# Filling matmuls around the score gradients of a backward loop, and earlier copies of turned weights in a forward loop

## Chip, cores, metric

One core of one Trainium2 chip. The metric is the device time of one execution in microseconds; lower is better.

## The reference, cut to what matters

A gated block with its gradients, bfloat16. The time goes into branch A, a segment-recurrent attention: 2048 tokens in 64 segments of 32; each segment attends to itself and to 8 memory rows, and the memory of the next segment is the output on those 8 rows. So both the forward pass and the backward pass are 64 steps in series.

```python
for s in range(n_seg):                         # 64, serial through mem
    xs = x[:, s * 32:(s + 1) * 32, :]
    h = jnp.concatenate([mem, xs], axis=1)     # 8 + 32 rows
    q, k, v = (einsum('btd,dhe->bhte', h, W) for W in (Wq, Wk, Wv))   # 32 heads x 128
    p = softmax(where(mask, q @ k.T * scale, -1e9))
    o = einsum('bhte,hed->btd', p @ v, Wo)
    mem = o[:, :8, :]
    outs.append(o[:, 8:, :])
# out = x + A(layernorm(x)) * silu(B(layernorm(x))), B a gated MLP;
# the kernel returns out and jax.vjp(...)(grad_out) for nine inputs
```

## The kernel before

A step computes only what lies on the memory rows. The work on the 32 tokens of earlier segments is put as fill into named gaps of the chain (W0, W1, G1 to G6), in units of four heads. `t` counts down in the backward loop; a step has 3, 3 or 2 units (2 where t mod 3 is 1). `WARM` says how many filling matmuls (128x512, result unused) a gap gets.

```python
# backward step, cut to the part that the change touches
packed_half(k, bA, gox, WoT, 0);  k.copy(sg[:, 0:512], bA[:], eng='v')
packed_half(k, bB, gox, WoT, 1);  k.copy(sg[:, 512:1024], bB[:], eng='s')
gap("W0")
# ... packed_sel into pg (bank C), copied to gmT
nc.sync.dma_start(k.GOS[...], sg[:])
gap("W1")
for h in range(H):                       # score gradients of the memory rows: 32 x 8 columns
    nc.tensor.matmul(psd[...], vT[:, h, :], gmT[...], start=True, stop=True)
# ... dPT and gOst copied on ScalarE
gap("G1")
gvT = gkv(1, gOst, bdP)                  # ends on VectorE
# ... softmax gradient on VectorE; loads(t - 1): vT, Pm, Qst (2) by nc.sync
gap("G2")
packed_out(k, pm, gvT, WvT, True, False) # value projection, 64 matmuls of 320 columns
# ... load_k(t - 1) by nc.sync; four stores of dS, two by nc.sync, two by nc.gpsimd
```
```python
def gap(g):                                              # backward fill
    if g == "W0":   ride_ld(t - 1); at(turn, t, 0)
    elif g == "W1": at(turn, t, 1); at(gmem_ld, t + 1, 2)   # turn needs gqv, gor
    # ... G1 to G3
    elif g == "G4": load_xp(t - 1); at(dsoft, t, 1); at(gmem_ld, t, 0)
    elif g == "G5": at(dprob, t, 2); at(gmem_ld, t, 1)
    # ... G6
    for i in range(WARM.get(g, 0)):
        nc.tensor.matmul((bA if g[0] == "W" or g == "G1" else bB)[:], k.ident[:], WqT[:, 0, 0:512], ...)

def ld(tl, qd):                        # the loads of one unit, four units ahead of use
    # ...
    for (a, b, src, w) in k.m_src(tl, "qv", c0, c0 + 512):          # L1174, w = 1: values
        (nc.gpsimd if early and w else nc.sync).dma_start(qv[a:b, w], ...)
    k.load_x(qv, nm, k.x_src(...), nc.sync)                          # L283
    k.load_x(gor, nm, k.g_src(...), ...)                             # L283, nc.sync
    nc.sync.dma_start(Pr[0:n], ...)                                  # L1177
```
```python
def gap(g):                                              # forward fill
    FILL(g, t, at, kbatch)                               # G3: maxima, exponentials of a unit
    for i in range(WARM.get(g, 0)):
        nc.tensor.matmul((bA if g == "G4" else bB)[:], k.ident[:], Wq[:, 0, 0:512], ...)
    if g in ("G2", "G5"):                                # turn a piece of a weight on TensorE
        wt["u"] = units.pop(0); wt["p"] = bview(bA if g == "G2" else bB, ...)
        wt["u"][0](wt["p"])
    if g == "G2": turned('v', nc.sync)                   # copy to wTst on VectorE, then store
    if g == "G6": turned('s', nc.sync)                   # the same on ScalarE
```

## Time and profile before

| | kernel before |
|---|---|
| time | 5631.07 us, median of four runs (5621.08 to 5634.92); the profiled one 5632.72 |
| TensorE busy | 88% of the span; next VectorE, 42% |
| forward loop, first to last step's start | 1354.6 us in 63 steps |
| backward loop, the same | 1260.6 us in 63 steps |
| half-clock stretches in the backward loop | 48, 187 us |

A half-clock stretch is a run of the clock record at half of full speed; a step with one at its value projection is called cold below, one without it warm. The two loops are read from the trace: the start of a step is its first matmul on `hx` (forward) or `gox` (backward). The prediction below shows the windows and the timeline. One view that it tells of only in words is the list of what TensorE waited for in the backward loop (columns: us in all, times, longest):

```profile
PE gbank L1090 <- DVE gmT L1085: 47.1, 57, 1.3
PE gbank L370 <- DVE gkv L1069: 27.4, 64, 0.4
```

These are the two idle places per step, some 0.8 us before the score gradients (L1090) and 0.4 before the value projection (L370), into which the change puts matmuls.

### The profile page before, as it was taken

The numbers are of one execution on the slowest core, as the hardware profiler recorded it, in microseconds if no ns is written. First come the engines' busy times: TensorE is split into PE (matmuls) and PEld (weight loads), VectorE is DVE, ScalarE is ACT, GpSimd is POOL, SyncE is SP. The second block draws the span as 40 slices with busy tenths as digits, with TensorE's granted clock in tenths as the row PEclk, the third lists the DMA queues.
The fourth block names the chain that finished last, engine by engine and source line by source line (L and its number), as shares of the span: only waits on it lengthen the run. The fifth ranks groups of instructions, "written<-read, shape, count | busy, mean of one in ns | idle before, by whom it ended". The sixth has DMA issues, their size and how long they took to land. (4 is left out here: it accounts for less than half of the span.)

```text
span 5628.0 us, 166669 instructions
## 1 busy us (share of the span) xinstructions
PE 4974.2 (88%) x67201; PEld 3195.0 (57%) x67486; DVE 2378.9 (42%) x7485; ACT 1834.3 (33%) x5040; POOL 1566.2 (28%) x2606
## 2 busy tenths in 40 slices
PE   4988889899888775889888896999999999999999
PEld 2554555555555453556666564665566556657565
DVE  5742555555555423444445442332233223311461
ACT  2432455555555522323333331332223212301111
POOL 0000244444444303333333332342234223300000
PEclk9999999999999787989999997999999999999999
DMA  7563455556555475666666664444344334456332
GB/s 256 181 205 94 140 163 168 167 166 170 161 157 151 113 208 164 177 185 182 188 179 179 174 173 114 120 100 98 84 108 102 99 87 102 122 163 228 102 118 91
DMA packets 1007171, 835.83 MB, mean 149 GB/s; under 512 B 505131, under 2 KB 894919, under 8 KB 1003083
## 3 DMA queue, kind: packets, MB, share of 16 engines
q1 hardware_dynamic: 760275, 570.63, 35.7%
q0 software_dynamic: 92560, 149.71, 9.5%
q10 hardware_dynamic: 153564, 104.81, 6.5%
q8 instruction: 532, 8.72, 0.6%
q14 instruction: 240, 1.97, 0.1%
HBM read 511.81 MB, written 324.39 MB: 149 GB/s over the span
## 5 line engine op out<-in xcount | busy, mean ns | idle before, releaser
L1460 PE MATMUL wg<-gr,hr 120*128 120x512 bf16 (+1 forms) x2640 | 588.1, 384 | 17.3 <-DVE dST L1392 13.2
L1438 PE MATMUL g<-w,gT 128*128 128x320 bf16 x3840 | 547.9, 299 | 0.0
L1460 PEld LDWEIGHTS <-hr 120*128 120x128 bf16 (+1 forms) x2640 | 257.8, 99 | 339.5 <-issue 45.9
L1438 PEld LDWEIGHTS <-gT 128*128 128x128 bf16 x3840 | 368.6, 98 | 136.0
L251 POOL DMA_DIRECT2D r<-GOS x256 | 143.1, 564 | 794.1 <-PE r6p L1402 720.5
L370 PEld LDWEIGHTS <-gkv 128*8 128x8 bf16 x8192 | 213.6, 98 | 152.1 <-DVE gkv L1069 34.4
L90 DVE CAST wgo<-wg 128x512 bf16<-128x512 f32 x72 | 47.5, 687 | 583.3 <-PE wg L1460 292.1
L351 PEld LDWEIGHTS <-hx 128*32 128x32 bf16 x7680 | 180.1, 96 | 182.7 <-issue 30.9
L90 DVE CAST stg<-bank 128x512 bf16<-128x512 f32 x256 | 177.0, 691 | 224.2 <-PE bank L351 213.6
L661 ACT ACTIVATE xP<-xsp,xnm 120x120 bf16<-120x120 f32 (+1 forms) x704 | 239.9, 375 | 32.1 <-issue 25.6
L370 PE MATMUL gbank<-WvT,gkv 128*8 128x320 bf16 x4096 | 225.6, 396 | 27.4 <-DVE gkv L1069 27.4
L1447 DVE TENSOR_TENSOR ghacc<-ghacc,g 128x320 f32<-128x320 f32 x240 | 117.0, 487 | 277.2 <-PE g L1438 277.2
L92 ACT CAST wgo<-wg 128x512 bf16<-128x512 f32 x48 | 25.8, 589 | 635.5 <-PE wg L1460 635.5
L1405 ACT CAST gr<-r6p 120x512 bf16<-120x512 f32 (+1 forms) x176 | 103.1, 586 | 361.2 <-PE r6p L1402 339.6
L1220 POOL DMA_DIRECT2D DSR<-gdS x176 | 101.6, 577 | 419.1 <-DVE gdS L1218 370.1
L710 POOL DMA_DIRECT2D OR<-xv x163 | 93.3, 572 | 444.2 <-ACT xv L709 280.8
L672 POOL TENSOR_TENSOR xP<-xP,xrz 120x480 bf16<-120x480 bf16 x163 | 161.6, 992 | 162.1 <-ACT xP L661 108.0
L92 ACT COPY gT<-t6g 128x960 bf16<-128x960 bf16 (+5 forms) x216 | 166.8, 792 | 118.4 <-PE t6g L1421 117.9
L370 PE MATMUL bank<-Wo,oTm 128*32 128x320 bf16 x4032 | 177.7, 330 | 14.7 <-DVE oTm L579 13.5
L1218 DVE SCALAR_TENSOR_TENSOR gdS<-gdp,Dx,gPr 120x120 bf16<-120x120 f32 (+1 forms) x680 | 182.9, 331 | 0.0
L536 DVE COPY vt<-stg 8x512 bf16<-8x512 bf16 x512 | 166.1, 324 | 31.8 <-ACT stg L92 24.9
L370 PEld LDWEIGHTS <-oTm 128*32 128x32 bf16 x4032 | 138.6, 105 | 64.9 <-issue 41.0
(360 smaller groups left out, 11094.4 us busy)
## 6 DMA issues: line engine op xcount, KB each, us to landing
QVS<-stg SPq DMA_DIRECT2D x128, 256.0 KB
gqv<-QVS SPq DMA_DIRECT2D x108, 192.0 KB
vTt<-VTD SPq DMA_DIRECT2D x64, 320.0 KB
VTD<-gvT POOLq DMA_DIRECT2D x168, 120.0 KB, 3.4
OR<-xv POOLq DMA_DIRECT2D x163, 120.0 KB, 2.8
DSR<-gdS POOLq DMA_DIRECT2D x168, 112.5 KB, 3.2
dS<-DSR SPq DMA_DIRECT2D x168, 112.5 KB
P<-PR SPq DMA_DIRECT2D x168, 112.5 KB
```

The lines of the kernel that those rows point to most:

```text
L90: return nc.vector.tensor_copy(out, in_)
L92: return nc.scalar.copy(out, in_)
L251: eng.dma_start(d, src if src.shape[0] > 1 else src[0])
L351: k.nc.tensor.matmul(bank[32 * g:32 * g + 32, :], x[:, dc, :], W[:, dc, c0:c0 + 512], start=(dc == 0), stop=(dc == k.DC - 1), tile_positio ...
L370: k.nc.tensor.matmul(pm[p0:p0 + nq, 0:320], x[:, h, :], W[:, h, 320 * b:320 * b + 320], start=(first and i == 0), stop=(last and i == 15), ...
L536: nc.vector.tensor_copy(vt[p0:p0 + 8, c0:c0 + 512], sv[32 * g:32 * g + 8, b * 512:(b + 1) * 512])
L661: nc.scalar.activation(Pb[0:n, j, 0:n], sp[0:n, j, :], ACT.Exp, bias=nmx[0:n, j:j + 1], scale=k.scale, accum_out=Z[0:n, j:j + 1])
L672: eng.tensor_tensor(Pb[0:n, :, 0:n], Pb[0:n, :, 0:n], bc_last(rz[0:n], n), ALU.mult)
L1218: nc.vector.scalar_tensor_tensor(dS[0:n, j, :], dp[0:n, j, :], Dx[0:n, j:j + 1], Pr[0:n, j, :], op0=ALU.subtract, op1=ALU.mult)
L1438: nc.tensor.matmul(pg[:], ring[:, i, j, r0:r0 + P], Ws[qd][i][:, j, 320 * h:320 * h + 320], start=(i == 0 and j == 0), stop=(i == 2 and j ...
L1447: nc.vector.tensor_tensor(a if qd < 7 else gx[:, 320 * h:320 * h + 320], a, g[h][:], ALU.add)
L1460: nc.tensor.matmul(accs[dc][:], hr[0:n, tl, dc * P:(dc + 1) * P], st["g", NTL * qd + tl, i][0:n, :], start=(tl == 0), stop=(tl == NTL - 1))
```

## The change

Its intent: keep TensorE busy enough ahead of the value projection that its clock isn't halved; and in the forward loop let the copies of the turned weights hold up neither the maxima on VectorE nor the key projection.

```diff
@@ forward loop
             def gap(g):
+                if g == "G6":
+                    turned('s', nc.sync)
                 FILL(g, t, at, kbatch)
+                if g == "G3":
+                    turned('v', nc.sync)
                 for i in range(WARM.get(g, 0)):
@@
-                if g == "G2":
-                    turned('v', nc.sync)
-                if g == "G6":
-                    turned('s', nc.sync)
             return gap
@@ backward loop
-        WARM = dict(G1=1, G5=2, G6=1)
+        WARM = dict(W1=3, G1=2, G2=2, G5=2, G6=1)
@@
-                    nc.tensor.matmul((bA if g[0] == "W" or g == "G1" else bB)[:], ...
+                    nc.tensor.matmul((bA if g in ("W1", "G1", "G2") else bB)[:], ...
```

More of the change, by code (lines that the diff above doesn't have):

```diff
@@ L1288, in gap @@
                 for i in range(WARM.get(g, 0)):
-                    nc.tensor.matmul((bA if g[0] == "W" or g == "G1" else bB)[:], k.ident[:], WqT[:, 0, 0:512], start=True, stop=True)
+                    nc.tensor.matmul((bA if g in ("W1", "G1", "G2") else bB)[:], k.ident[:], WqT[:, 0, 0:512], start=True, stop=True)
             return gap
```

## The prediction

> **What bounds the kernel now.** I read the page first: TensorE is busy 88% of the span, no other engine over 42%. The change touches two loops of 64 steps each. By the first and last matmuls on their inputs, the forward loop runs from 543 to about 1918 us, mean step 21.50 us; the backward loop from 2205 to about 3486, mean step 20.01. A step is a serial chain TensorE, VectorE, ScalarE, TensorE, with filling work between its links, so I asked for the granted clock by stretch.
>
> ```profile
> core 0: us, PE busy (x) PEld busy (x) DVE busy (x) ACT busy (x) POOL busy (x), PEclk, DMA share, GB/s
> 500.00:2000.00 1500.00, 1303.84 (x23456) 820.18 (x23582) 803.08 (x2348) 786.38 (x2643) 580.27 (x829) 0.95 0.55 155
> 2200.00:3480.00 1280.00, 1134.43 (x24248) 754.07 (x24379) 592.46 (x2777) 379.29 (x1231) 420.64 (x768) 0.92 0.62 169
> ```
>
> The backward loop has the lower clock, 0.92. Two neighbouring steps of it, as windows, then what differs between them in the timeline of TensorE:
>
> ```profile
> 3046.15:3064.97 18.82, 16.77 (x386) 11.63 (x389) 8.60 (x41) 6.38 (x20) 6.62 (x13) 1.00 0.70 184
> 3064.97:3085.23 20.26, 18.38 (x395) 12.36 (x398) 10.30 (x53) 6.68 (x22) 7.13 (x14) 0.92 0.67 191
> ```
> ```profile
> 3050.77 1.00 PE L1090 MATMUL gbank<-gmT,vTt 128*40 128x8 bf16 x32 [0.89 <-DVE gmT L1085]
> ...
> 3053.36 2.35 PE L370 MATMUL gbank<-WvT,gkv 128*8 128x320 bf16 x64 [0.43 <-DVE gkv L1069]
> ```
> ```profile
> 3072.19 3.75 PE L370 MATMUL gbank<-WvT,gkv 128*8 128x320 bf16 x64 [0.43 <-DVE gkv L1069]
> ```
>
> The reader is to see that the value projection (WvT) takes 2.35 us in a step at full clock and 3.75 in the next, and that this is nearly the whole difference between 18.82 and 20.26. Step by step in the trace, all warm steps are 18.83 us (18.48 where t mod 3 is 1), most cold ones 19.95 to 20.52. The clock record has 48 half-clock stretches in this loop, 187 us in all; nearly all begin 6.0 to 7.7 us after the step's start, where the value projection is. Windows of 3.41 us around one of them:
>
> ```profile
> 2709.89:2713.30 3.41, 3.34 (x65) 2.10 (x58) 2.70 (x14) 1.20 (x4) 1.43 (x3) 1.00 0.52 151
> 2713.30:2716.71 3.41, 2.25 (x57) 1.90 (x55) 1.25 (x3) 2.30 (x8) 2.58 (x5) 1.00 0.89 233
> 2716.71:2720.13 3.42, 3.19 (x52) 1.68 (x56) 3.21 (x19) 0.00 (x0) 0.00 (x0) 0.50 0.95 315
> ```
>
> The window before the cold one holds 57 matmuls, but nearly all small: 32 of 8 columns (score gradients), some of 24 to 128. In the forward loop one step of the commonest kind reads:
>
> ```profile
> 1092.04 0.49 DVE L90 COPY wTst<-bank 128x640 bf16<-128x640 bf16 x1 [0.27 <-PE bank L295]
> 1092.45 0.65 DVE L655 TENSOR_REDUCE xmx<-xsp 120x4 f32<-120x480 f32 x1
> ```
> ```profile
> 1094.41 2.45 PE L370 MATMUL bank<-Wo,oTm 128*32 128x320 bf16 x64 [0.43 <-DVE oTm L579]
> ...
> 1101.69 0.40 PE L351 MATMUL bank<-Wk,hx 128*32 128x512 bf16 x4 [0.26 <-ACT wTst L92]
> ```
> ```profile
> 1097.33 0.27 ACT L661 ACTIVATION_READ_ACCUMULATOR xP<-xsp,xnm 120x1 f32 x1
> 1097.62 0.29 ACT L381 COPY fup<-bank 64x160 f32<-64x160 f32 x1
> ```
>
> The weight copy holds VectorE while the maxima (xmx), whose scores are long there, wait. That delays the exponentials (xP) on ScalarE, and they delay the fold copy (fup) on which the next step depends. The last line of TensorE waits for the second weight piece's copy.
>
> [...] the granted clock is 1.0 or 0.5 only, in multiples of 3.41 us. [...] Here two fillers of the forward loop start 0.22 to 0.23 us apart. [...] here a filler's record is 0.38 long at that spacing, so I count starts. [...] the reduction above begins right at the copy's end.
>
> **Part 1, the fillers.** Per backward step three are added ahead of the score gradients (place W1), one after them (G1, now two), two ahead of the value projection (G2, none before): 6 a step, 384 in the loop, each 128x512; the order of instructions on TensorE confirms the count, and nothing else moves there.
>
> Does it warm the clock? For every 3.41 us window I added up columns over granted clock, overlaps counted once. Windows that precede a cold one lie under about 0.35 of the window, others above, in both loops (5 of 293 windows backward and 6 of 378 forward are out of order). This is an estimate from the trace[...]. Sliding a window over a backward step, the share sinks to 0.16 and stays under the threshold for starts over some 2.0 of 3.41 us. Three fillers are 3 x 0.213 = 0.64 us, 0.19 of a window; two more 0.12. Put into the idle time at W1 and G2 they lift the least share in ordinary steps to 0.35 to 0.42, and the one at G1 adds 0.06 to some. So nearly every one of these cold windows should go.
>
> What it saves: the 64 steps take about 1280.5 us; 43 x 18.83 + 21 x 18.48 = 1197.8; difference 82.7. Of it 18 lie in seven odd steps: the first, two around a late transfer (gride, about 2430 us), the last four, which have little fill. There I take 5. So 65 + 5 = 70 saved.
>
> What it costs: idle before the score gradients is 0.88 to 1.06 us from the last matmul's columns; three fillers need 0.10 + 3 x 0.22 = 0.76 and fit. Before the projection it is 0.59; two need 0.54 and just fit: say 0.03 x 64 = 2 us. At G1 there is room for one only: two end at about 6.4 us after the step's start, the matmuls that follow start at 6.34 now, so 0.07 x 64 = 4.5. In some four steps the fill before W1 ends late and the fillers delay: 4 x 0.65 = 2.6. They write bank A, whose last reader finished long before, so there is no new wait. Net -61 us.
>
> **Part 2, the forward copies.** The first piece's copy goes behind the maxima of two softmaxes: these start 0.40 us earlier (0.76 in steps with t mod 3 = 1, where the copy also waited for its transposes). The exponentials can't start before the probabilities' copy (PTm) on the same engine, so gain 0.33 and 0.65; the fold copy, now 1.06 us after the last projection matmul where 0.38 is usual, follows them. Against it: two fillers ahead of the output projection write the bank that the copy reads, so must now wait for it; the projection starts 0.17 later, 0.21 earlier, 0.15 later in the three kinds of step. In the third kind, with two softmaxes, the exponentials do not bind, and the 0.15 is lost. Sum of three steps: -0.33 - 0.65 + 0.15 = -0.83.
> The second piece's copy at once: the second half of the key projection starts 0.43 to 0.64 us after the first's last matmul, where 0.19 is the usual gap of four; -0.24 - 0.45 - 0.45 = -1.14 (less, -0.81, in the last third). Some 20 threes of 1.97 or 1.64 give -37 us. But the fillers now leave the window that is poorest in columns: by the same sliding sum its share falls to 0.26 in the first kind and 0.31 in the third, some five more cold windows of 1.5 us: +8. Net -29.
>
> **Sum.** 5632.7 - 61 - 29 = 5543 us, 1.6% faster.
>
> **Rivals.** (a) The fillers lengthen the chain more than they warm it: at half clock three last 1.3 us and overrun the 0.88. For it: a busy TensorE at 88%. Against: 17 steps have no cold window, and the idle time is measured in them. It would give 5600 to 5640. (b) Faster backward steps run into transfers: share 0.62 of the queues, loads with one buffer (values, keys). For it: one late transfer already. Against: neighbouring warm steps, up to three, show no wait. It would give back 20 to 30 us: 5568. (c) The forward copies bring more cold windows than they save, as the steps may lock to six windows (20.48 us), as backward steps do now: +25, 5568. (d) Both parts come in full and no extra cold windows come: 5632.7 - 75 - 40 = 5518, just over 2%.
>
> **Range and chances.** Part 1 gives 45 to 75, part 2 gives 5 to 42, the odd transfers and run spread (5621 to 5635) some 7 either way: 5510 to 5582. Over 2% means under 5520, which needs (d): 0.17. Slower by 2% needs a mechanism that I don't see: 0.01; the rest, 0.82, is within 2%.
>
> **What would show it.** Right: backward clock about 0.97 or more, fewer than 15 half-clock stretches there, value projection 2.35 us in ordinary steps, steps of 18.5 to 18.9, score gradients still 4.6 us after the step's start. Forward: fold copy 0.3 to 0.65 us earlier in two of three steps, and no wait of the key projection for the weight copy. Wrong: steps warm but longer than 18.9 (a), new waits for transfers (b), forward clock under 0.95 (c), or the fillers there with the projection still at 3.7 us[...].

## The result, and the profile after

5564.02 us median (5556.07 to 5579.3, four runs) against 5631.07 (5621.08 to 5634.92, four runs): ratio 0.9887, 95% interval 0.9861 to 0.9913. It counts as the same, being within 2%, and is 1.1% faster. Ratios here are the mean time of one kernel's runs over that of the other's of the same rounds, so not quite the ratio of the medians.

By stretch, from the traces of both (us):

| | before | after | difference | predicted |
|---|---|---|---|---|
| forward loop | 1354.6 | 1323.4 | -31 | -29 |
| backward loop | 1260.6 | 1227.8 | -33 | -61 |
| between the loops | 308.4 | 303.1 | -5 | 0 |
| after the loops | 2161.9 | 2167.0 | +5 | 0 |
| half-clock stretches, backward | 48 (187 us) | 8 (56 us) | | under 15 |

The 5 us between and after the loops, where the kernels are the same, are within what all the traces show there (302.4 to 312.0 and 2160.5 to 2172.2 us).

The windows of the kernel after (columns as in the prediction; the second to last triple is clock, DMA share, GB/s):

```profile
500.00:2000.00 1500.00, 1321.61 (x23715) 817.80 (x23841) 807.03 (x2367) 794.88 (x2657) 580.75 (x829) 0.95 0.56 160
2160.00:3420.00 1260.00, 1156.07 (x24695) 759.39 (x24882) 591.06 (x2783) 381.40 (x1233) 424.14 (x775) 0.97 0.64 173
```

The forward step that answers to the one in the prediction (that one began at 1078.04, this one at 1066.51), then the first line of the step after it:

```profile
1080.60 0.65 DVE L655 TENSOR_REDUCE xmx<-xsp 120x4 f32<-120x480 f32 x1
...
1081.39 0.49 DVE L90 COPY wTst<-bank 128x640 bf16<-128x640 bf16 x1
...
1082.45 2.36 PE L370 MATMUL bank<-Wo,oTm 128*32 128x320 bf16 x64
...
1085.20 0.29 ACT L381 COPY fup<-bank 64x160 f32<-64x160 f32 x1
...
1087.74 2.34 PE L351 MATMUL bank<-Wk,hx 128*32 128x512 bf16 x40
```

The weight copy now comes behind the maxima, the fold copy 18.69 us into the step in place of 19.58, and the key projection runs in one piece (x40, no wait for `wTst`). Of the 0.89 us of the fold copy, 0.37 lie between the end of the output projection and the copy, near the predicted 0.33; the rest lies ahead, 0.32 of it already where the query projection starts (3.42 us into the step before, 3.10 now). So the forward part shows what was predicted.

The clock of the backward loop rose from 0.92 to 0.97. An ordinary step in the timeline of TensorE (it starts at 3053.17):

```profile
3057.79 1.00 PE L1090 MATMUL gbank<-gmT,vTt 128*40 128x8 bf16 x32 [0.25 <-DVE gmT L1085]
3060.43 2.35 PE L370 MATMUL gbank<-WvT,gkv 128*8 128x320 bf16 x64
```

The score gradients start 4.62 us into the step as before, the value projection takes 2.35. Ordinary steps are 18.90 us, or 18.54 where t mod 3 is 1. So the clock part worked as planned. But the sum of 63 such steps is 1183 us and the loop took 1228: 45 us lie in excess of it. Where, the waits of TensorE in the backward loop show:

```profile
PE gbank L1289 <- issue: 11.7, 67, 0.3
PE gvpt L1186 <- DMA gqv<-QVS: 9.7, 7, 3.9
PE gbank L1090 <- DVE gmT L1085: 7.6, 22, 0.7
PE gvpt L1186 <- DMA gqv<-QVX: 5.5, 3, 2.4
```

The idle time before L1090 went from 47.1 to 7.6 us, taken by the fillers (L1289). New are waits of up to 3.9 us for the loads of `gqv`, in the fill at W1 (`turn`, L1186). By steps, 38 us of the 45 lie in twelve such steps, ten of them with t mod 3 = 1; the other 7 in two steps around a late transfer that the kernel before has too. One such step, TensorE:

```profile
3029.97 2.34 PE L351 MATMUL gbank<-WoT,gox 128*32 128x512 bf16 x40
...
3032.67 0.59 PE L359 MATMUL gbank<-sel,gstg 128*128 128x32 bf16 x8
3034.72 0.37 PE L1186 MATMUL gvpt<-ident,gqv 120*128 120x120 bf16 x4 [1.46 <-DMA gqv<-QVX]
...
3036.86 1.24 PE L1090 MATMUL gbank<-gmT,vTt 128*40 128x8 bf16 x32
...
3041.00 3.26 PE L370 MATMUL gbank<-WvT,gkv 128*8 128x320 bf16 x64
```

TensorE idles 1.46 us for `gqv`, then does the fillers though the score gradients are overdue (they start 6.89 us into the step), and the half clock is back from 3036.08 to 3042.91 us: 3.26 us for the value projection. The step took 23.20 us at a mean granted clock of 0.85; the ordinary one above had 1.00. Of the loop's waits for `gqv` in this fill, five, 1.46 to 3.91 us long, have the half clock begin during them or within 1.4 us of their end; of the others, up to 1.58, none has. The issues of SyncE (SPq) in the same stretch, second column the length of the issue:

```profile
3027.77 1.01 SPq L1046 DMA_DIRECT2D xp<-GXP  x1
3028.88 0.59 SPq L1236 DMA_DIRECT2D GXP<-gks  x1
3029.57 2.08 SPq L1174 DMA_DIRECT2D gqv<-QVS  x4
3031.69 0.60 SPq L283 DMA_DIRECT2D gqv<-QVX  x1
3032.39 0.54 SPq L283 DMA_DIRECT2D gor<-GOS  x1
3032.97 0.43 SPq L1177 DMA_DIRECT2D gPr<-PR  x1
```

The load that TensorE waits for was issued at 3031.69, 1.7 us after the step's start, and was in use 3.0 us later, which is the usual time (from issue to the last update of its semaphore, the median of the 56 loads `gqv<-QVX` of the loop is 2.9 us, before and after alike). It is late because it was issued late, and SyncE issues one transfer right after another: from 3019.38 us on, no gap between two of its records in this stretch is over 0.2 us, so it wasn't held up by a wait either. Here the next record starts 0.04 to 0.10 us after the last, once 0.17. Counted over the loop, SyncE issues 1725 transfers, 27.4 a step, and they take 944 us plus 115 between them (0.55 us each and 0.07 between), 1059 of 1228 us. Before it was 936 + 114 = 1050 of 1261. By kind of step (t mod 3 = 0, 1, 2; t from 6 to 59 without the two around the late transfer) this was 15.7, 18.5 and 18.7 us in the kernel before, against warm steps of 18.83, 18.48 and 18.83: two of three steps leave it next to no slack. So my theory after the traces: **the change made SyncE's issuing the second bound of the backward loop.** The rival: the transfers themselves come late, the same bytes in shorter steps.

### The profile page after: what moved, and what is told of

It reads as the page before. It is cut to its first block, busy times and chain, and to the rows that moved or that the text cites. A ratio compares the mean times of both kernels' runs of the same rounds, so it can differ in the third digit from the quotient of the medians.

```text
span 5565.9 us, 167384 instructions
## 1 busy us (share of the span) xinstructions
PE 4988.2 (90%) x67526; PEld 3177.3 (57%) x67870; DVE 2372.9 (43%) x7485; ACT 1836.6 (33%) x5040; POOL 1567.2 (28%) x2606
## 5 line engine op out<-in xcount | busy, mean ns | idle before, releaser
L370 PEld LDWEIGHTS <-gkv 128*8 128x8 bf16 x8192 | 190.9, 88 | 104.3 <-DVE gkv L1069 24.6
L1421 PE MATMUL t6g<-ident,gr 120*128 120x120 bf16 (+1 forms) x2112 | 171.1, 220 | 3.6 <-DVE wgo L90 3.1
L1289 PE MATMUL gbank<-WqT,ident 128*128 128x512 bf16 x453 | 156.4, 394 | 19.5 <-issue 11.7
```

The costliest lines, as they stand in the source:

```text
L370: k.nc.tensor.matmul(pm[p0:p0 + nq, 0:320], x[:, h, :], W[:, h, 320 * b:320 * b + 320], start=(first and i == 0), stop=(last and i == 15), ...
L1421: nc.tensor.transpose(pt[:, i - i0, j, :], st["g", u, i][0:n, j * P:(j + 1) * P], k.ident[0:n, 0:n])
```

## The experiments

Every run was correct. e1 to e4 ran on one chip, r_after and e6 to e8 on a second, e10 to e13 on a third, each group with runs of the kernel before among them.

### The two parts apart: e1_fill_only, e2_fwd_only

```diff
 e1: kernel before, with only
+        WARM = dict(W1=3, G1=2, G2=2, G5=2, G6=1)      and the bank bA for W1, G1, G2
 e2: kernel after, with
+        WARM = dict(G1=1, G5=2, G6=1)
```

> The backward part of the change alone (three fillers at W1, one more at G1, two at G2); the forward loop is that of the kernel before. If the two parts add up, this saves what the backward loop saved in the trace of the whole change: 33 us of its loop, so about 5599 us, ratio 0.994, with late loads of gqv and gor stalling TensorE in some ten steps as in the whole change. If the stalls came from something that the forward part left behind, they would be absent here and the saving would be the 61 us of the prediction: 5571 us, ratio 0.989.

> The forward part alone (both copies of the turned weight pieces moved to G3 and G6 ahead of the fillers' place); the backward fillers are those of the kernel before. Expected from the trace of the whole change: the forward loop 31 us shorter, mean step 21.0 us in place of 21.5, the rest as before: about 5601 us, ratio 0.9945. A rival, that the forward loop gains only because the memory is left in another state, has no place to show itself, so a ratio over 0.998 would mean that the forward gain is given back later.

Measured: e1 5591.11 us, ratio 0.993 (0.9917 to 0.9943); its backward loop took 1237.3 us with the same waits for `gqv`, 23 us less than before where 33 were expected (the profiled run, 5597.07 us, is the slowest of the six). e2 5606.99 us, 0.9965 (0.9947 to 0.9983), forward loop 1324.1, backward loop 1261.6 with 51 half-clock stretches. So the fillers save some 39 us by themselves (32 to 47), the copies some 20 (10 to 30). Within the intervals they add up to the 64 us of the first comparison (the repeat below, r_after, gave 41), and the stalls come with the fillers alone. The copies gave less in time than the 31 us that the first pair of traces showed.

### Which fillers: e4_w1_only

```diff
-        WARM = dict(W1=3, G1=2, G2=2, G5=2, G6=1)
+        WARM = dict(W1=3, G1=1, G5=2, G6=1)
```

> The whole change less the fillers at G1 (one) and G2 (two) of the backward loop: only the three at W1 are kept. If the three at W1 are what keeps the clock up, the half-clock stretches stay as few (under 12) and the steps are 0.07 us shorter: about 5559 us, ratio 0.9875. If those at G1 and G2 are needed too, the half clock comes back at the value projection in most steps: its matmuls' stretch is over 2.5 us again, up to 48 stretches, and most of the backward gain is lost: 5590 us or more, ratio over 0.992.

Measured: 5583.55 us (5562.18 to 5606.32), 0.9919 (0.9896 to 0.9941). Ordinary steps were 18.83 and 18.48 us, 0.07 less, as expected; half-clock stretches 16, over the 12 expected, so the three at W1 do most of the work, but not all: four of the 16 (t = 62, 54, 24, 18) lie in steps that are 1.7 us longer, as the cold steps before were, and none of the kernel after does. Whether the other three pay can't be told from the times: the stalls spread the runs over 44 us.

### Fewer issues on SyncE, first try: e3_loads_act

```diff
-            nc.sync.dma_start(vT[:], ...)          # and Pm, and the two of Qst
+            nc.scalar.dma_start(vT[:], ...)
```

> The whole change, with the four loads of a step that the stalls of the backward loop waited for or queued behind (values, probabilities and the two halves of the query state) issued by ScalarE in place of SyncE. Theory: SyncE is busy issuing for 14 to 17 us of an 18.5 to 18.9 us step, one issue after another, and its loads come late in the steps with the most issues. Then taking four issues a step (some 2 to 3 us) from it makes the stalls vanish: about 35 us less than the whole change, 5530 to 5540 us, ratio 0.982 to 0.984, and no wait of TensorE for gqv or gor over 5 us in the whole loop. Rival: the transfers themselves are late, since the same bytes move in shorter steps; then nothing changes: 5564 us, ratio 0.988, the same stalls. Third: ScalarE[...] holds up its own work behind these issues: ratio over 0.990.

Measured: 5597.46 us, 0.9937 (0.9924 to 0.9951), the stalls still there. Taken alone this speaks against the theory. But the waits of SyncE (SPq) in its trace are new:

```profile
SPq L283 <- DMA vTt<-VTD: 57.0, 25, 5.3
SPq L1174 <- DMA vTt<-VTD: 39.1, 18, 3.6
```

SyncE waits 96 us for loads of `vTt`, which no data of its own loads depends on. In the records of the kernel after, the transfers of SyncE and ScalarE (4763 and 606) count on the same eight semaphores, those of GpSimd (2092) on eight others. Each of the 5361 issues of SyncE and ScalarE that follow another on their semaphore began after that one's last update, at the least 0.016 us after; the kernel before has the same. So ScalarE's issues, which come when ScalarE gets to them, now held SyncE up: all its waits for transfers in the loop are 179 us, in the kernel after 18. The run doesn't tell the theories apart, nor whether ScalarE's own work was held up as well, the third guess.

### Fewer and more issues on SyncE, second try: r_after, e6_v_pool, e7_more_sp, e8_dsm_pool

All are the kernel after; r_after is it unaltered.

```diff
 e6: the value halves of gqv by GpSimd
-                (nc.gpsimd if early and w else nc.sync).dma_start(qv[a:b, w], ...)
+                (nc.gpsimd if w else nc.sync).dma_start(qv[a:b, w], ...)
 e7: all stores of dS by SyncE;  e8: all by GpSimd
-                        (nc.sync, nc.gpsimd)[a].dma_start(k.DSR[...], dS[...])
+                        (nc.sync, nc.sync)[a].dma_start(...)          # e7
+                        (nc.gpsimd, nc.gpsimd)[a].dma_start(...)      # e8
```

> The whole change once more, unaltered, as the yardstick for the three beside it and to narrow its ratio: 0.9887 again, within 0.987 to 0.9905, and the same steps stalled as in its first trace (those with t mod 3 = 1, for gqv and gor).

> The whole change, with the value halves of the gqv loads of the backward loop issued by GpSimd in place of SyncE (about 3.7 of some 28 issues a step). The run with four loads moved to ScalarE did not settle the matter: ScalarE shares its eight completion semaphores with SyncE, and SyncE then waited for loads that ScalarE issued late. GpSimd has eight of its own. Theory that SyncE's issuing is the bound (17 us of issues and 2 us between them in an 18.5 us step): it loses 2 us a step and the stalls go: the backward loop 25 to 38 us shorter than in the whole change, ratio 0.982 to 0.985. Rival, that the transfers are late on the way: the same bytes, no change, 0.988 to 0.99. Second rival, that GpSimd issues them later than SyncE did, behind its own waits: more stalls, over 0.991.

> The whole change with the suspected cost increased: the two stores of score gradients that GpSimd issued in each step are issued by SyncE as well, so two issues more a step (some 1.3 us with the time between them), the same bytes and the same transfers. If SyncE's issuing is the bound, the steps that now just fit do not fit any more: 25 to 60 us more than the whole change, ratio 0.993 to 1.0, and more waits of TensorE for gqv and gor. If the transfers are the bound, no change: 0.988 to 0.99.

> The opposite of the run beside it: the two stores of score gradients that SyncE issued in each step go to GpSimd, which issues all four: two issues less on SyncE, 1.3 us a step, the same bytes. If SyncE's issuing is the bound, about half of the stalls go or more: 15 to 30 us less than the whole change, ratio 0.983 to 0.986. If the transfers are the bound: 0.988 to 0.99.

Measured:

| | issues of SyncE a step | their time and the time between, in the loop | backward loop | time | ratio (95%) |
|---|---|---|---|---|---|
| e6_v_pool | 23.7 | 914 us | 1193.6 us | 5536.68 us | 0.9828 (0.9813 to 0.9843) |
| e8_dsm_pool | 25.4 | 986 | 1202.0 | 5554.53 | 0.9857 (0.9841 to 0.9873) |
| r_after | 27.4 | 1062 | 1244.7 | 5592.88 | 0.9928 (0.9912 to 0.9944) |
| e7_more_sp | 29.4 | 1156 | 1308.4 | 5654.03 | 1.0026 (1.0003 to 1.0048) |

The same bytes move in all four; only the issuer differs, and with it the queue and the completion semaphores (in the trace of the kernel after SyncE's issues add up to 570 MB, ScalarE's to 105, GpSimd's to 149; its page has 571, 105 and 150 MB on three queues). The time follows the number of issues on SyncE, over 117 us, as expected (e7 lost 61 us against r_after where 25 to 60 were expected). In e7 the change's whole gain is gone. What TensorE waited for in the backward loop of e7:

```profile
PE gvpt L1186 <- DMA gqv<-QVS: 33.7, 14, 4.9
...
PE gvpt L1186 <- DMA gqv<-QVX: 21.4, 9, 4.8
```

In e6 the lines of L1186 are not in that list at all. The step that stalled above, in e6, on TensorE and then on SyncE:

```profile
3010.12 2.34 PE L351 MATMUL gbank<-WoT,gox 128*32 128x512 bf16 x40
...
3013.26 0.37 PE L1186 MATMUL gvpt<-ident,gqv 120*128 120x120 bf16 x4
...
3017.40 2.35 PE L370 MATMUL gbank<-WvT,gkv 128*8 128x320 bf16 x64
```
```profile
3006.54 1.04 SPq L1174 DMA_DIRECT2D gqv<-QVS  x2
3007.62 0.61 SPq L283 DMA_DIRECT2D gqv<-QVX  x1
```

The load is issued 2.5 us before the step's start in place of 1.7 us after it, and the step takes 18.55 us. The rival falls by the windows of e6 and e7 as well:

```profile
2160.00:3380.00 1220.00, 1136.51 (x24629) 749.98 (x24819) 589.19 (x2777) 379.37 (x1231) 556.01 (x1003) 0.99 0.68 179
```
```profile
2160.00:3500.00 1340.00, 1179.37 (x24516) 767.48 (x24700) 593.97 (x2807) 385.08 (x1240) 345.81 (x647) 0.94 0.60 164
```

The DMA engines moved 179 GB/s at a share of 0.68 in the kernel that doesn't stall and 164 at 0.60 in the one that stalls most. They were not the limit. Nor do the other two things that differ explain it: the loads `gqv<-QVX` took longer to land in e6 (median 3.3 us from issue) than in r_after (3.1), and SyncE's waits for transfers, the shared semaphores among them, are 20 us in the whole loop of r_after and 15 in e6. The moved loads came no sooner by GpSimd (median 3.4 us from issue to landing in e6, against 2.5 for `gqv<-QVS` by SyncE in r_after). The time saved on the sequencer was 2.3 us a step (against r_after, 233 issues: 124 us of records and 24 us between, over 63 steps), and it was worth 56 us, or 27 against the first measurement of the same kernel, on another chip.

r_after missed its expectation: 0.9928 where the first measurement of the same kernel gave 0.9887. Its stalls cost 62 us in the trace, not 45, and lie partly in other steps. In the first trace 18 us of waits for `gqv` and `gor` went with the 38 us lost, as the half clock came with the five waits told of above, so small differences may decide. Whether the other chip or chance makes it, these runs don't settle. Without the stalls it hardly varies: 5530.87 to 5540.09 in e6.

### Was it in the way before? e10_before_v_pool; and the filler at G1: e11_best

```diff
 e10: kernel before with the edit of e6
 e11: e6 with
-        WARM = dict(W1=3, G1=2, G2=2, G5=2, G6=1)
+        WARM = dict(W1=3, G1=1, G2=2, G5=2, G6=1)
```

> The kernel before, with only the value halves of the gqv loads issued by GpSimd. If SyncE became a bound only through the change (its 14 to 17 us of issues fit a 20 us step with a half-clock window, not one of 18.5 to 18.9 us), this gains nothing by itself: ratio 0.997 to 1.001, some 45 to 50 half-clock stretches still in the backward loop. If the loads were in the way before as well, it gains 10 to 25 us of its own: 0.995 to 0.998, and the 56 us by which this edit shortened the changed kernel are only partly the change's gain given back.

> The whole change with the value halves on GpSimd and one filler at G1 in place of two. The prediction put the second filler at G1 at 0.07 us a step on the path, 4.5 us in all, and the run with the fillers at W1 alone had warm steps shorter by 0.07. So warm steps of 18.83 and 18.48 us in place of 18.90 and 18.54, if the clock stays up without it: 5532 us, ratio 0.982, against 0.9828 of the run with two. If that filler is needed in some steps, half-clock stretches come back, over 8 in the backward loop, and the ratio is 0.983 or more.

Measured: e10 5629.25 us, 0.9987 (0.9973 to 1.0001), 47 half-clock stretches, backward loop 1256.4 us. The edit that is worth 56 us to the changed kernel is worth nothing certain to the kernel before. So SyncE was no bound there; its work fits into steps of 20 us. e11: 5542.15 us, 0.983 (0.9814 to 0.9845), no gain over e6 within the intervals. Its ordinary steps are 18.87 and 18.52 us with 4 half-clock stretches, so by this trace the second filler at G1 isn't needed and costs 0.03 us a step, not 0.07; with e4 (18.83) the two at G2 cost 0.04.

### The two copies apart: e12_s_only, e13_v_only

Both on e6, so that the backward loop stays out of it.

```diff
 e12: first piece's copy back at G2
-                if g == "G3":
-                    turned('v', nc.sync)
+                if g == "G2":                        # at the end of gap
+                    turned('v', nc.sync)
 e13: second piece's copy back at the end of G6
-                if g == "G6":
-                    turned('s', nc.sync)             # before FILL
+                if g == "G6":                        # at the end of gap
+                    turned('s', nc.sync)
```

> The forward part halved, on the kernel with the value halves on GpSimd (whose backward loop has hardly any stalls that vary): the second piece's copy at once (G6), the first piece's copy back at its old place (G2). The prediction gave the second piece 24 us of the forward loop and the first 17 us, less 8 for more half-clock windows. So 12 to 17 us more than with both: ratio 0.985 to 0.986; the wait of the key projection for the copy gone, the fold copy again 1.06 us behind the last projection matmul in steps with t mod 3 = 0 and 1. If the half-clock windows come from this move, the forward loop has 18 or 19 of them here too.

> The other half, on the same kernel: the first piece's copy moved (G3), the second's back at its old place. By the prediction's terms 24 us more than with both, less what the half-clock windows took: ratio 0.985 to 0.987; the fold copy early (0.6 to 0.7 us behind the last projection matmul), the key projection again waiting for the second piece's copy by 0.43 to 0.64 us. If the half-clock windows come from the other move, the forward loop has about 15 of them or fewer.

Measured: e12 5532.93 us (5531.41 to 5534.28), 0.9815 (0.9802 to 0.9828), **the fastest of all**; e13 5553.04 us, 0.9846 (0.983 to 0.9863). Forward loops: 1326.4 us in e12, 1343.6 in e13, 1324.9 in e6 with both, 1354.6 and 1350.2 in the kernel before and e10 with neither. e12 was expected 12 to 17 us slower than e6, at 0.985 to 0.986; it isn't. The second piece's copy carries the gain; the first's adds nothing that can be seen. By kind of step, t mod 3, steps 6 to 57 of the forward loop, median and mean length in us (the median is an ordinary step, the mean has the half-clock windows in it):

| | 0 | 1 | 2 |
|---|---|---|---|
| e12, second piece only | 21.07, 21.04 | 21.70, 21.54 | 20.50, 20.46 |
| e6, both | 20.76, 20.54 | 21.14, 21.37 | 20.68, 21.15 |

Moving the first piece as well gains 0.31 and 0.56 us in ordinary steps of the first two kinds and loses 0.18 in the third, as the fillers now wait for the copy (23.7 us in 60 steps in e6; no such wait before). But the means of the three sum to 63.06 with both and 63.04 with one: in the third kind the output projection falls into a half-clock window more often. The step lengths are one trace each, but the half clock is not: in the ten traces with the first piece moved (e13 among them) 9 to 15 half-clock stretches begin in steps of the third kind, in the four without (before, e1, e10, e12) 4 to 7. So they come from this move, which delays the fillers.

## Why the prediction was right or wrong

The class was right, and 5564 us lies in the range of 5510 to 5582, 21 us above the 5543. That is partly luck: the repeat, 5593 us, lies outside it, and part 1 missed its own range of 45 to 75 (33 in the trace; 39 in time alone, e1). Two figures of the prediction are loose, without consequence: 1918 and 3486 are the first step's start and 64 mean steps, while the last matmuls on the inputs start at 1905 and 3468; and the upper end of the range, 5582, leaves out the 7 us of run spread. Point by point:

- **The clock is the limit of backward steps, and six fillers cure it**: right. 48 half-clock stretches became 8 (13 in r_after, 4 in e6), the projection 2.35 us, the clock 0.97. That it follows streamed columns, 0.35 of a window, was an estimate, with a column counted as 0.417 ns at full clock (in the trace before, matmuls start 216 ns apart with 512 columns and 136 with 320); it told correctly that three fillers at W1 do most (e4), but no run was made to test the figure. Counted in the same way in the backward loop of the kernel after, the 7 windows at full clock that precede a cold one have 0.15 to 0.28, the other 335 have 0.29 or more.
- **What the fillers cost**: nearly right. Predicted 0.10 us an ordinary step (0.03 at G2, 0.07 at G1); measured 0.07 (0.04 and 0.03).
- **"Net -61 us" for part 1**: the step that failed. The loop lost 33 us in the first trace, and the fillers alone saved 39 in time (e1). The saving of 70 was there in ordinary steps; what was left out was that shorter steps make the loads late: 38 us in the first trace. With SyncE relieved the same fillers give -67 (1260.6 to 1193.6, e6), or -63 against the kernel before with the same relief (e10), so the working up to that term held.
- **Rival (b)** came true in size, 20 to 30 us given back and 5568, against 5564 measured, but by another mechanism than it named: not the transfers, whose share is higher in the faster kernel, but the time to issue them. The evidence that I set against it, that neighbouring warm steps show no wait, was the error. At most three warm steps in a row let SyncE fall behind only a little, and each 20 us step let it catch up; this is an argument, not shown. I counted the DMA engines' share and never SyncE's, whose issues aren't counted as busy. Yet the sum was in the trace: 1050 us of issuing, against the 1198 us of all-warm steps that the prediction itself worked out, is 0.88 on average, with some 26 issues in steps with t mod 3 = 0 and 29 in the others.
- **Part 2, -29**: right in the first trace (-31), high by a third in the time (e2: -20). The mean of nine forward loops with both copies moved is 1328.3 us (1319.8 to 1336.8), of three with neither 1350.2 (1345.7 to 1354.6): -22. By the prediction's sum the second piece was worth -20 (20 threes of 1.14 us, 0.81 in the last third; the 24 in the expectations of e12 and e13 leaves the last third out); measured -24 (e12: 1326.4 against 1350.2, one trace). The term of the first, -17 + 8, was mis-sized: e13 against e10 shows -7 alone, and beside the second piece's it is about nil. Its gain in ordinary steps was near (0.69 us in three steps where 0.83 were predicted, some 14 us in the loop), but the half clock takes it all back, not 8 of it, though the extra windows are as few as predicted (18.6 half-clock stretches in the forward loop, mean of the nine, against 14).
- **Rivals (a), (c), (d)**: the fillers lengthen an ordinary step by 0.07 us, so (a) didn't come; the forward clock stayed at 0.95, so (c) came only in the weak form just told; (d), 5518, wasn't reached even by the best kernel, 5533.

What stays open: how much the first piece's copy costs or gains by itself within some 10 us (nine loops with the same code spread over 17), and why the same changed kernel gave 0.9887 once and 0.9928 another time.

## What to carry to other kernels

When a change shortens the steps of a loop, set the work of every queue against the new step, the issuing of transfers too: the busy shares of these profiles don't count it, so add up the issue records and the time between them. A list of waits in the slow kernel doesn't show the next bound, since the slack that is to be removed hides it; here 2 us of issues a step, moved to another engine, were worth nothing certain before the change and 56 us after it. When issues are moved, look which completion semaphores the other engine uses (96 us of SyncE's waits in e3 were for loads that ScalarE issued; e6, which moved other loads to GpSimd, had 15 us of waits for transfers in all). And leave stalls no room in a loop where the half clock was seen to come with them: here 18 us of waits went with 38 us lost.
